# Static expert capacity of 608 rows in place of 640 in a fused attention, feed-forward and mixture-of-experts kernel

## The chip, the cores and the metric

The kernel runs on one core of one Trainium2 chip. The metric is the device time of one execution in microseconds, as the median of several runs. The profile is of one further execution on the same kind of core.

## The reference

Three stages follow on each other. First a landmark attention over 4 batches, 8 heads, 576 positions and head width 64 (32 landmarks, six steps of an iterative inverse). Its output, as 2304 tokens of width 512, goes through a feed-forward layer with an ELU (512 to 2048 to 512). The result `x` goes through eight experts, of which each token takes the two with the largest noisy logits:

```python
logits = x @ w_gate
noise_scale = np.log1p(np.exp(x @ w_noise))
noisy_logits = logits + noise_scale * noise
top2 = np.argpartition(-noisy_logits, 2, axis=1)[:, :2]
...
for e in range(E):
    for k in range(2):
        mask = top2[:, k] == e
        h = np.maximum(x[mask] @ w1[e], 0.0)
        out[mask] += top2_w[mask, k, None] * (h @ w2[e])
```

`w1[e]` is 512 x 1024 and `w2[e]` is 1024 x 512, with E = 8. 2304 tokens with two experts each make 4608 rows, 576 per expert on average; how many an expert gets depends on the inputs.

## The kernel before

All matrix products run in f16 with a split: a value is kept as a high half and a low half, and a product is three matmuls (high by high, high by low, low by high) summed in PSUM.

**Order of the work.** The Tile framework places the instructions, but from the attention to the end of expert 0 their order on every engine is written out by hand in the string ORDER, inside a manual schedule (line 1025). Experts 1 to 7 follow in a second manual schedule, the loop at line 1028. SP issues the plain DMAs and the transposing DMAs, POOL the indirect ones (gather and scatter by a list of row numbers).

**Routing.** As the tokens of a chunk come out of the feed-forward layer, the two experts of each token and its position in each expert's list are computed, and `RS` (line 837) scatters the token's row (512 values as two f16 halves, then token number, first expert and the two weights) into the DRAM table `xs`. Each expert has a section of STRIDE rows there. `fill_xs` (line 715) has earlier written zero rows with dummy token numbers over the first CAP = 640 rows of each section, so an expert always handles 640 rows, real ones and dummies. `count` holds the real row counts, `blocks` the number of blocks of 128 rows that lie past CAP.

**One expert.** `fetch_x` (line 869) brings its rows in transposed, as `XT[e]` (two halves, each 128 partitions by 4 by 640 columns), and their weights and token numbers as `WS[e]`. `weigh_x` (line 881) makes integer token numbers `TK[e]` and the right weight of each row. `ew_load` (line 853) loads expert weights two experts ahead in eight pieces of 512 KB; `ew_split` (line 858) splits each piece on ACT (high) and DVE (low).

The first layer is `e1` (line 913). For each of eight blocks `f` of 128 hidden columns it does two parts of the rows, 320 each: `e1_mm` (line 895) runs 12 matmuls (3 passes by 4 slices of the width) whose stationary operand is a 128 x 128 block of `w1` and whose moving operand is the part's columns of `XT`. Then `e1_hi` (line 903) applies ReLU on ACT and writes the high half of the hidden tile `EH[e, f]`, and `e1_lo` (line 908) makes the low half on DVE. Expert 0 is cut otherwise: its rows 0 to 383 (EARLY) are certain to be filled before the last chunk is routed, so its parts are 384 and 256 rows (`XP`, `EPART`, lines 1001 and 1002), and the second part is done after the last rows have been scattered.

The second layer is `e2` (line 939), over five blocks `j` of 128 rows. `e2_mm` (line 922) runs 24 matmuls (8 blocks f by 3 passes), in which the stationary operand is the 128 rows of the hidden tile and the moving operand is 512 columns of `w2`:

```python
for f in range(8):
    for i, (x, y) in enumerate(((0, 0), (0, 1), (1, 0))):
        T.matmul(p, EH[e, f][:, x, 128 * j:128 * j + 128], W2T[e][y][:, f, :],
```

`e2_out` (line 929) scales the 128 x 512 result by the row weights on ACT, and `e2_add` (line 933) adds it to the DRAM table `acc` with an indirect DMA that accumulates. The last expert is different: `last_base` (line 954) copies `acc` to the output and gathers the sums of its own rows, and each block is then weighted and added to those on DVE (line 946) and scattered straight into the output (line 948).

**The end.** From `peak` (line 1046) on, a branch handles experts with more than CAP real rows, 128 rows at a time, weights loaded and split anew. With no such expert the branch is skipped.

Of the kernel before, what the change touches and what calls it, by code (L numbers as in the profile page):

```python
# [8 lines left out]
F32 = mybir.dt.float32  # L9
F16 = mybir.dt.float16  # L10
I32 = mybir.dt.int32
U32 = mybir.dt.uint32
AF = mybir.ActivationFunctionType
ALU = mybir.AluOpType
# [6 lines left out]
DM, DFF = 512, 2048  # L21
NE, FE = 8, 1024
NT = B * S
CAP = 640
EARLY = 384
PITCH = 520
STRIDE = NT + 128
NT5 = 6
# [153 lines left out]
def attn_ffn_moe_kernel(ctx: ExitStack, tc: tile.TileContext, q: bass.AP, k: bass.AP, v: bass.AP,  # L182
                        w_in: bass.AP, w_out: bass.AP, w_gate: bass.AP, w_noise: bass.AP,
                        noise: bass.AP, w1: bass.AP, w2: bass.AP, out: bass.AP):
    nc = tc.nc
# [5 lines left out]
    cst = ctx.enter_context(tc.tile_pool(name="cst", bufs=1))  # L191
    sb = ctx.enter_context(tc.tile_pool(name="sb", bufs=1))
    ps = ctx.enter_context(tc.tile_pool(name="ps", bufs=1, space=bass.MemoryType.PSUM))
# [6 lines left out]
    V, A, G, T = nc.vector, nc.scalar, nc.gpsimd, nc.tensor  # L200
    PASSES = ((0, 0), (0, 1), (1, 0))

    def half(name):
        return sb.tile([128, 4096], F16, tag="half", bufs=12, name=name)
# [10 lines left out]
    def act(o, i, f=AF.Copy, **kw):  # L215
        return A.activation(o, i, f, **kw)  # L216
# [468 lines left out]
    blocks = cst.tile([128, NE], I32, name="blocks")  # L685
    counti = cst.tile([128, NE + 1], I32, name="counti")
    spacer = cst.tile([1, 1], F32, name="spacer")
    xs = dr.tile([NE * STRIDE, PITCH], F32, name="xs")
    acc = dr.tile([NT + 128, DM], F32, name="acc")

    wgf = {}
    zrow = cst.tile([128, PITCH], F32, name="zrow")
# [20 lines left out]
        V.tensor_scalar(zrow[:, DM:DM + 1], tokid[:, 0:1], float(NT), None, op0=ALU.add)  # L713

    def fill_xs(e):
        nc.sync.dma_start(xs[e * STRIDE:e * STRIDE + CAP].rearrange("(j p) c -> p j c", p=128),
                          zrow[:, None, :].to_broadcast([128, CAP // 128, PITCH]))

    def fill_acc(i):
        a = acc.rearrange("(j p) c -> p j c", p=128)[:, 5 * i:min(5 * i + 5, 19)]  # L720
# [15 lines left out]
    def routing(c):  # L736
# [75 lines left out]
        def RF():  # L812
# [16 lines left out]
            if c == LAST:  # L829
# [3 lines left out]
                V.tensor_copy(counti, count)  # L833
                V.tensor_scalar(blocks, count[:, :NE], float(CAP), float(127 - CAP), op0=ALU.max, op1=ALU.add)
                V.tensor_scalar(blocks, blocks, 7, None, op0=ALU.logical_shift_right)
# [13 lines left out]
    W1T, W2T, XT, WS, TK = {}, {}, {}, {}, {}  # L849
# [18 lines left out]

    def fetch_x(e, s0, s1_):
        if e not in XT:  # L870
            XT[e] = [half(f"xT{e}{i}")[:, :4 * CAP].rearrange("p (d n) -> p d n", d=4) for i in range(2)]
            WS[e] = cst.tile([128, CAP // 128, 4], F32, tag="ws", bufs=2, name=f"ws{e}")
            TK[e] = cst.tile([128, CAP // 128], I32, tag="tk", bufs=2, name=f"tk{e}")
        j0, j1 = s0 // 128, s1_ // 128
        src = xs[e * STRIDE + s0:e * STRIDE + s1_]
        for i in range(2):
            nc.sync.dma_start_transpose(out=XT[e][i][:, :, s0:s1_],
                                        in_=src[:, DM // 2 * i:DM // 2 * (i + 1)].bitcast(F16))
        nc.sync.dma_start(WS[e][:, j0:j1], src[:, DM:DM + 4].rearrange("(j p) c -> p j c", p=128))

    def weigh_x(e, s0, s1_):
        j0, j1 = s0 // 128, s1_ // 128
        w = WS[e][:, j0:j1]
        V.tensor_copy(TK[e][:, j0:j1, None], w[:, :, 0:1])
        V.scalar_tensor_tensor(w[:, :, 2:3], w[:, :, 1:2], float(e), w[:, :, 2:3], op0=ALU.is_equal,
                               op1=ALU.mult)
        V.scalar_tensor_tensor(w[:, :, 3:4], w[:, :, 1:2], float(e), w[:, :, 3:4], op0=ALU.not_equal,
                               op1=ALU.mult)
        V.tensor_tensor(out=w[:, :, 2:3], in0=w[:, :, 2:3], in1=w[:, :, 3:4], op=ALU.add)

    EH = {}
# [3 lines left out]
    def e1_mm(e, f, s0, n):  # L895
        tag = ("l1", "a")[f % 2 if e == 0 else s0 > 0]
        p = EP[e, f, s0] = ps.tile([128, 512], F32, tag=tag, bufs=2, name=f"eh{e}_{f}_{s0}")[:, :n]
        for i, (x, y) in enumerate(((0, 0), (0, 1), (1, 0))):
            for d in range(4):
                T.matmul(p, W1T[e][x][:, d, 128 * f:128 * f + 128], XT[e][y][:, d, s0:s0 + n],  # L900
                         start=(i == 0 and d == 0), stop=(i == 2 and d == 3))

    def e1_hi(e, f, s0, n):
        if (e, f) not in EH:
            EH[e, f] = sbe.tile([128, 2, CAP], F16, tag="hT", bufs=8, name=f"eh{e}_{f}")
        act(EH[e, f][:, 0, s0:s0 + n], EP[e, f, s0], AF.Relu)
# [6 lines left out]
    def e1(e, f, parts):  # L913
        for s0, n in parts:
            for g in (e1_mm, e1_hi, e1_lo):
                g(e, f, s0, n)

    outs, BASE = [], {}

    EY = {}  # L920

    def e2_mm(e, j):
        p = EY[e, j] = ps.tile([128, 512], F32, tag="y", bufs=3, name=f"ey{e}_{j}")
        for f in range(8):
            for i, (x, y) in enumerate(((0, 0), (0, 1), (1, 0))):
                T.matmul(p, EH[e, f][:, x, 128 * j:128 * j + 128], W2T[e][y][:, f, :],  # L926
                         start=(f == 0 and i == 0), stop=(f == 7 and i == 2))

    def e2_out(e, j):
        o = EO[e, j] = sb.tile([128, DM], F32, tag="t5", bufs=NT5, name=f"eo{e}_{j}")  # L930
        act(o, EY[e, j], scale=WS[e][:, j, 2:3])

    def e2_add(e, j):
        nc.gpsimd.indirect_dma_start(out=acc[:, :], out_offset=bass.IndirectOffsetOnAxis(ap=TK[e][:, j:j + 1], axis=0),  # L934
                                     in_=EO[e, j], in_offset=None, compute_op=ALU.add)

    EO = {}

    def e2(e, j):
        e2_mm(e, j)  # L940
        if e < NE - 1:
            e2_out(e, j)
            e2_add(e, j)
            return
        o = sb.tile([128, DM], F32, tag="t5", bufs=NT5, name=f"eo{e}_{j}")
        V.scalar_tensor_tensor(o, EY[e, j], WS[e][:, j, 2:3], BASE[j], op0=ALU.mult, op1=ALU.add)
        G.memset(spacer, 0.0)
        n = nc.gpsimd.indirect_dma_start(out=out[:, :], out_offset=bass.IndirectOffsetOnAxis(ap=TK[e][:, j:j + 1], axis=0),  # L948
                                         in_=o, in_offset=None, bounds_check=NT - 1, oob_is_err=False)
        for x in outs:  # L950
            tc.declare_no_dep(n.ins, x.ins, reason="a row of its own")
        outs.append(n)

    def last_base(e):
        nc.sync.dma_start(out, acc[:NT])
        for j in range(CAP // 128):
            BASE[j] = sb.tile([128, DM], F32, tag="t5", bufs=NT5, name=f"base{j}")
            nc.gpsimd.indirect_dma_start(out=BASE[j], out_offset=None, in_=acc[:, :],
                                         in_offset=bass.IndirectOffsetOnAxis(ap=TK[e][:, j:j + 1], axis=0))


    def step(g, n=1):
# [26 lines left out]
    def pool():  # L989
# [6 lines left out]
           "consts": route_consts, "cl": route_loads, "PD": ew_load, "P": ew_split,  # L996
           "LX": lambda e, p: fetch_x(e, *XP[e][p]), "LW": lambda e, p: weigh_x(e, *XP[e][p]),
           "E1": lambda f, p: e1_mm(0, f, *EPART[p]), "EA": lambda f, p: e1_hi(0, f, *EPART[p]),
           "EV": lambda f, p: e1_lo(0, f, *EPART[p]), "E2": lambda j: e2_mm(0, j), "EO": lambda j: e2_out(0, j),
           "ES": lambda j: e2_add(0, j), "pool": pool, "F": warm}  # L1000
    XP = {0: ((0, EARLY), (EARLY, CAP)), 1: ((0, CAP),)}
    EPART = ((0, EARLY), (EARLY, CAP - EARLY))
    for n in "XTSHO":
        CMD[n] = lambda c, f, *e, n=n: elu(c, f, n, *e)
# [22 lines left out]
    manual.enter_context(tc.manual_schedule(engines={ET.PE, ET.DVE, ET.Activation, ET.Pool, ET.SP}))  # L1027
    for e in range(1, NE):
        if e + 1 < NE:
            fetch_x(e + 1, 0, CAP)  # L1030
        if e == NE - 1:
            last_base(e)
        for f in range(8):
            e1(e, f, [(0, CAP // 2), (CAP // 2, CAP // 2)])
            if e + 1 < NE:
                for part in range(2):
                    ew_split(e + 1, f, part)
            if e + 2 < NE:
                ew_load(e + 2, f)
        for j in range(5):  # L1040
            e2(e, j)
            if j == 1 and e + 1 < NE:
                weigh_x(e + 1, 0, CAP)
    manual.close()

    peak = nc.values_load(counti[0:1, NE:NE + 1], min_val=0, max_val=NT)  # L1046
    with tc.If(peak > CAP):
        ef = cst.tile([128, 1], F32, name="ef")
        V.memset(ef, -1.0)
        with tc.For_i(0, NE, 1) as e:  # L1050
            V.tensor_scalar(ef, ef, 1.0, None, op0=ALU.add)
            nb = nc.values_load(blocks[0:1, bass.ds(e, 1)], min_val=0, max_val=(NT - CAP) // 128)
            with tc.If(nb > 0):
                ce = nc.values_load(counti[0:1, bass.ds(e, 1)], min_val=0, max_val=NT)
                nc.sync.dma_start(xs[bass.ds(e * STRIDE + ce, 128)], zrow)
# [2 lines left out]
                for src, dst, kn, nm, scale in ((w1, w1x, 1, "a", S_W1), (w2, w2x, 2, "b", S_W2)):  # L1058
                    for j in range(4):
# [6 lines left out]
                                               op1=ALU.subtract)  # L1066
                with tc.For_i(0, nb, 1) as i:
# [5 lines left out]
                    tk = cst.tile([128, 1], I32, name="tkx")  # L1073
# [3 lines left out]
                                           op1=ALU.mult)  # L1077
                    V.tensor_tensor(out=wt[:, 2:3], in0=wt[:, 2:3], in1=wt[:, 3:4], op=ALU.add)
                    base = sb.tile([128, DM], F32, tag="t5", bufs=NT5, name="basex")
# [5 lines left out]
                    for f in range(8):  # L1085
                        p = ps.tile([128, 512], F32, tag="l1", bufs=2, name=f"hx{f}")[:, :128]
# [6 lines left out]
                    p = ps.tile([128, 512], F32, tag="y", bufs=3, name="yx")  # L1093
# [36 lines left out]
```

## Time and profile before

| | |
|---|---|
| median of 3 runs | 853.97 us (853.81 to 853.98) |
| profiled execution, its own time | 854.51 us |
| its span, first to last instruction | 852.8 us |
| mean granted TensorE clock over the span | 0.977 |
| instructions in the span | 15270 |

The time of an execution and the span of its profile differ by what lies around the first and last instruction, here 1.7 us. PE is TensorE's matmuls and PEld its weight loads, which overlap them; DVE, ACT and POOL are the vector, scalar and GpSimd engines, and SPq is the queue that issues DMAs. In a group of the profile "busy" is the union of its instructions' times, the mean is that of one instruction, and the idle time is that of the engine just before them, with what ended it. A matmul's mean is longer than the distance from one to the next, because matmuls are pipelined. "128*128 128x320" is a stationary operand of 128 x 128 and a moving one of 320 columns. The timeline merges neighbours of the same kind: start, length from the first start to the last end, and count.

### The profile page before, as it was taken

The numbers are of one execution on the slowest core, as the hardware profiler recorded it, in microseconds if no ns is written. First come the engines' busy times: TensorE is split into PE (matmuls) and PEld (weight loads), VectorE is DVE, ScalarE is ACT, GpSimd is POOL, SyncE is SP. The second block draws the span as 40 slices with busy tenths as digits, with TensorE's granted clock in tenths as the row PEclk, the third lists the DMA queues.
The fourth block names the chain that finished last, engine by engine and source line by source line (L and its number), as shares of the span: only waits on it lengthen the run. The fifth ranks groups of instructions, "written<-read, shape, count | busy, mean of one in ns | idle before, by whom it ended". The sixth has DMA issues, their size and how long they took to land. (4 is left out here: it accounts for less than half of the span.)

```text
span 852.8 us, 15270 instructions
## 1 busy us (share of the span) xinstructions
PE 807.9 (95%) x6113; PEld 470.0 (55%) x6114; DVE 449.1 (53%) x984; ACT 409.2 (48%) x749; POOL 294.5 (35%) x313
## 2 busy tenths in 40 slices
PE   7768989999999999999999999999999999999994
PEld 6653345555654556654456664746557465564752
DVE  7989999876684974636461340613416043160210
ACT  5677668776757576565532341514325143241200
POOL 4556755665552454354430212021020210202311
PEclk9769999999999999999999999999999999999997
DMA  9868699597486513341659876565646747403730
GB/s 341 300 155 192 181 324 343 138 222 222 90 208 122 193 46 110 107 109 49 181 151 171 142 189 84 148 149 111 171 67 163 144 113 185 51 2 40 221 110 35
DMA packets 137227, 129.64 MB, mean 152 GB/s; under 512 B 100597, under 2 KB 103669, under 8 KB 137056
## 3 DMA queue, kind: packets, MB, share of 16 engines
q1 hardware_dynamic: 128432, 107.32, 47.5%
q0 software_dynamic: 8720, 21.30, 11.8%
q8 instruction: 49, 0.80, 0.4%
q14 instruction: 26, 0.21, 0.1%
HBM read 70.71 MB, written 40.42 MB: 130 GB/s over the span
## 5 line engine op out<-in xcount | busy, mean ns | idle before, releaser
L900 PE MATMUL eh<-xT,w 128*128 128x320 f16 (+2 forms) x1536 | 210.6, 299 | 0.0
L926 PE MATMUL ey<-w,eh 128*128 128x512 f16 x960 | 208.8, 379 | 0.0
L671 PE MATMUL y<-wout,g 128*128 128x512 f16 x864 | 207.0, 379 | 0.7 <-POOL g L664 0.7
L910 DVE SCALAR_TENSOR_TENSOR eh<-eh,eh 128x320 f16<-128x320 f32 (+2 forms) x128 | 62.0, 489 | 236.8 <-ACT eh L216 236.8
L900 PEld LDWEIGHTS <-w 128*128 128x128 f16 x1536 | 150.1, 98 | 59.7
L926 PEld LDWEIGHTS <-eh 128*128 128x128 f16 x960 | 93.9, 98 | 111.7
L934 POOL DMA_INDIRECT acc<-eo,tk x35 | 54.6, 1561 | 290.6 <-ACT eo L216 157.0
L664 POOL TENSOR_TENSOR g<-e,g 128x384 f16<-128x384 f32 (+2 forms) x96 | 100.6, 1051 | 129.1 <-ACT g L216 114.0
L671 PEld LDWEIGHTS <-g 128*128 128x128 f16 x864 | 81.3, 99 | 93.5 <-issue 8.3
L633 PE MATMUL h<-AT,G 128*128 128x192 f16 (+3 forms) x768 | 110.1, 289 | 8.1 <-DVE e L659 5.0
L216 ACT ACTIVATE eh<-eh 128x320 f16<-128x320 f32 (+2 forms) x128 | 55.5, 437 | 126.6 <-PE eh L900 117.1
L633 PEld LDWEIGHTS <-G 128*128 128x128 f16 x768 | 64.2, 99 | 49.6 <-issue 11.2
L867 DVE SCALAR_TENSOR_TENSOR w<-ew,w 128x1024 f16<-128x1024 f32 x64 | 78.2, 1224 | 22.0 <-ACT w L216 22.0
L216 ACT ACTIVATE eo<-ey,ws 128x512 f32<-128x512 f32 x35 | 23.8, 688 | 135.0 <-PE ey L926 135.0
L659 DVE SCALAR_TENSOR_TENSOR e<-e,h 128x384 f32<-128x384 f32 (+2 forms) x96 | 52.7, 550 | 32.1 <-ACT e L216 21.4
L216 ACT ACTIVATE e<-h 128x384 f32<-128x384 f32 (+2 forms) x96 | 47.2, 493 | 46.3 <-PE h L633 22.4
L216 ACT ACTIVATE w<-ew 128x1024 f16<-128x1024 f32 x64 | 67.0, 1048 | 0.0
L216 ACT ACTIVATE g<-e 128x384 f16<-128x384 f32 (+2 forms) x96 | 49.7, 519 | 32.6 <-DVE e L659 18.0
L839 POOL DMA_INDIRECT xs<-rows,pos x36 | 36.5, 1014 | 31.5 <-DVE count L831 20.5
L216 ACT ACTIVATE e<-e 128x384 f32<-128x384 f32 (+2 forms) x57 | 29.9, 524 | 0.9
L655 DVE TENSOR_SCALAR e<-e 128x384 f32<-128x384 f32 (+2 forms) x39 | 19.2, 492 | 16.8 <-ACT e L216 16.7
L608 DVE SCALAR_TENSOR_TENSOR G<-pg,G 128x512 f16<-128x512 f32 x32 | 21.6, 690 | 7.8 <-ACT G L216 7.8
(199 smaller groups left out, 753.8 us busy)
## 6 DMA issues: line engine op xcount, KB each, us to landing
ew<-in_moe_w_dram SPq DMA_DIRECT2D x64, 512.0 KB, 3.7
xs<-zrow SPq DMA_DIRECT2D x8, 1300.0 KB, 19.2
wo<-in_moe_w_out_dram SPq DMA_DIRECT2D x16, 512.0 KB, 4.5
wi<-in_moe_w_in_dram SPq DMA_DIRECT2D x16, 512.0 KB, 8.3
q<-in_q_dram SPq DMA_DIRECT2D x8, 576.0 KB, 7.1
k<-in_k_dram SPq DMA_DIRECT2D x8, 576.0 KB, 6.3
v<-in_v_dram SPq DMA_DIRECT2D x4, 1152.0 KB, 13.0
out_dram<-acc SPq DMA_DIRECT2D x1, 4608.0 KB
```

The source lines that it names most:

```text
L216: return A.activation(o, i, f, **kw)
L608: V.scalar_tensor_tensor(gt[:, g, 1, fs], X["pg"][g], S_G, gt[:, g, 0, fs], op0=ALU.mult, op1=ALU.subtract)
L633: T.matmul(p[:, c0:c0 + n], GT[b, f // 8][:, g, x, fs], AT[b][:, g, y, o:o + n], start=(i == 0), stop=(i == 5))
L659: V.scalar_tensor_tensor(x[1], x[1], x[2], x[0], op0=ALU.mult, op1=ALU.max)
L664: G.tensor_tensor(out=HT[c, f][:, 1], in0=x[1], in1=HT[c, f][:, 0], op=ALU.subtract)
L671: T.matmul(YP[c, t], h[:, x, 128 * t:128 * t + 128], WOUT[f][:, y], start=(f == 0 and i == 0), stop=(f == 15 and i == 2))
L839: n = nc.gpsimd.indirect_dma_start(out=xs[:, :], out_offset=bass.IndirectOffsetOnAxis(ap=R["pos"][:, i // 2, i % 2:i % 2 + 1], axis=0), in ...
L867: V.scalar_tensor_tensor(dst[1][:, ks, :], t, scale, dst[0][:, ks, :], op0=ALU.mult, op1=ALU.subtract)
L900: T.matmul(p, W1T[e][x][:, d, 128 * f:128 * f + 128], XT[e][y][:, d, s0:s0 + n], start=(i == 0 and d == 0), stop=(i == 2 and d == 3))
L910: V.scalar_tensor_tensor(h[:, 1, s0:s0 + n], EP[e, f, s0], 0.0, h[:, 0, s0:s0 + n], op0=ALU.max, op1=ALU.subtract)
L926: T.matmul(p, EH[e, f][:, x, 128 * j:128 * j + 128], W2T[e][y][:, f, :], start=(f == 0 and i == 0), stop=(f == 7 and i == 2))
L934: nc.gpsimd.indirect_dma_start(out=acc[:, :], out_offset=bass.IndirectOffsetOnAxis(ap=TK[e][:, j:j + 1], axis=0), in_=EO[e, j], in_offset= ...
```

## The change

The capacity CAP becomes 608. A new constant PAD = 640 takes its place where rows are filled, fetched, weighed and transposed, so that these handle as many rows as before. The two parts of a first layer are 304 columns each for experts 1 to 7 and 384 and 224 for expert 0. The five blocks of a second layer stay; a new function `live(j)` gives the rows of block j, which are 128 for the first four and 96 for the last. The last block's matmuls take 96 columns of the hidden tile as stationary operand, and its eviction, its scatter and, for the last expert, its gather handle 96 rows. The hidden tile has 608 columns. The branch at the end is taken if an expert has more than 608 rows, and its bound on blocks is rounded up.

```diff
--- before.py
+++ after.py
@@ -21,7 +21,8 @@
 DM, DFF = 512, 2048
 NE, FE = 8, 1024
 NT = B * S
-CAP = 640
+CAP = 608
+PAD = 640
 EARLY = 384
 PITCH = 520
 STRIDE = NT + 128
@@ -713,8 +714,8 @@
         V.tensor_scalar(zrow[:, DM:DM + 1], tokid[:, 0:1], float(NT), None, op0=ALU.add)
 
     def fill_xs(e):
-        nc.sync.dma_start(xs[e * STRIDE:e * STRIDE + CAP].rearrange("(j p) c -> p j c", p=128),
-                          zrow[:, None, :].to_broadcast([128, CAP // 128, PITCH]))
+        nc.sync.dma_start(xs[e * STRIDE:e * STRIDE + PAD].rearrange("(j p) c -> p j c", p=128),
+                          zrow[:, None, :].to_broadcast([128, PAD // 128, PITCH]))
 
     def fill_acc(i):
         a = acc.rearrange("(j p) c -> p j c", p=128)[:, 5 * i:min(5 * i + 5, 19)]
@@ -868,9 +869,9 @@
 
     def fetch_x(e, s0, s1_):
         if e not in XT:
-            XT[e] = [half(f"xT{e}{i}")[:, :4 * CAP].rearrange("p (d n) -> p d n", d=4) for i in range(2)]
-            WS[e] = cst.tile([128, CAP // 128, 4], F32, tag="ws", bufs=2, name=f"ws{e}")
-            TK[e] = cst.tile([128, CAP // 128], I32, tag="tk", bufs=2, name=f"tk{e}")
+            XT[e] = [half(f"xT{e}{i}")[:, :4 * PAD].rearrange("p (d n) -> p d n", d=4) for i in range(2)]
+            WS[e] = cst.tile([128, PAD // 128, 4], F32, tag="ws", bufs=2, name=f"ws{e}")
+            TK[e] = cst.tile([128, PAD // 128], I32, tag="tk", bufs=2, name=f"tk{e}")
         j0, j1 = s0 // 128, s1_ // 128
         src = xs[e * STRIDE + s0:e * STRIDE + s1_]
         for i in range(2):
@@ -919,19 +920,23 @@
 
     EY = {}
 
+    def live(j):
+
+        return min(128, CAP - 128 * j)
+
     def e2_mm(e, j):
-        p = EY[e, j] = ps.tile([128, 512], F32, tag="y", bufs=3, name=f"ey{e}_{j}")
+        p = EY[e, j] = ps.tile([128, 512], F32, tag="y", bufs=3, name=f"ey{e}_{j}")[:live(j)]
         for f in range(8):
             for i, (x, y) in enumerate(((0, 0), (0, 1), (1, 0))):
-                T.matmul(p, EH[e, f][:, x, 128 * j:128 * j + 128], W2T[e][y][:, f, :],
+                T.matmul(p, EH[e, f][:, x, 128 * j:128 * j + live(j)], W2T[e][y][:, f, :],
                          start=(f == 0 and i == 0), stop=(f == 7 and i == 2))
 
     def e2_out(e, j):
-        o = EO[e, j] = sb.tile([128, DM], F32, tag="t5", bufs=NT5, name=f"eo{e}_{j}")
-        act(o, EY[e, j], scale=WS[e][:, j, 2:3])
+        o = EO[e, j] = sb.tile([128, DM], F32, tag="t5", bufs=NT5, name=f"eo{e}_{j}")[:live(j)]
+        act(o, EY[e, j], scale=WS[e][:live(j), j, 2:3])
 
     def e2_add(e, j):
-        nc.gpsimd.indirect_dma_start(out=acc[:, :], out_offset=bass.IndirectOffsetOnAxis(ap=TK[e][:, j:j + 1], axis=0),
+        nc.gpsimd.indirect_dma_start(out=acc[:, :], out_offset=bass.IndirectOffsetOnAxis(ap=TK[e][:live(j), j:j + 1], axis=0),
                                      in_=EO[e, j], in_offset=None, compute_op=ALU.add)
 
     EO = {}
@@ -942,10 +947,10 @@
             e2_out(e, j)
             e2_add(e, j)
             return
-        o = sb.tile([128, DM], F32, tag="t5", bufs=NT5, name=f"eo{e}_{j}")
-        V.scalar_tensor_tensor(o, EY[e, j], WS[e][:, j, 2:3], BASE[j], op0=ALU.mult, op1=ALU.add)
+        o = sb.tile([128, DM], F32, tag="t5", bufs=NT5, name=f"eo{e}_{j}")[:live(j)]
+        V.scalar_tensor_tensor(o, EY[e, j], WS[e][:live(j), j, 2:3], BASE[j], op0=ALU.mult, op1=ALU.add)
         G.memset(spacer, 0.0)
-        n = nc.gpsimd.indirect_dma_start(out=out[:, :], out_offset=bass.IndirectOffsetOnAxis(ap=TK[e][:, j:j + 1], axis=0),
+        n = nc.gpsimd.indirect_dma_start(out=out[:, :], out_offset=bass.IndirectOffsetOnAxis(ap=TK[e][:live(j), j:j + 1], axis=0),
                                          in_=o, in_offset=None, bounds_check=NT - 1, oob_is_err=False)
         for x in outs:
             tc.declare_no_dep(n.ins, x.ins, reason="a row of its own")
@@ -953,10 +958,10 @@
 
     def last_base(e):
         nc.sync.dma_start(out, acc[:NT])
-        for j in range(CAP // 128):
-            BASE[j] = sb.tile([128, DM], F32, tag="t5", bufs=NT5, name=f"base{j}")
+        for j in range(PAD // 128):
+            BASE[j] = sb.tile([128, DM], F32, tag="t5", bufs=NT5, name=f"base{j}")[:live(j)]
             nc.gpsimd.indirect_dma_start(out=BASE[j], out_offset=None, in_=acc[:, :],
-                                         in_offset=bass.IndirectOffsetOnAxis(ap=TK[e][:, j:j + 1], axis=0))
+                                         in_offset=bass.IndirectOffsetOnAxis(ap=TK[e][:live(j), j:j + 1], axis=0))
 
 
     def step(g, n=1):
@@ -998,7 +1003,7 @@
            "E1": lambda f, p: e1_mm(0, f, *EPART[p]), "EA": lambda f, p: e1_hi(0, f, *EPART[p]),
            "EV": lambda f, p: e1_lo(0, f, *EPART[p]), "E2": lambda j: e2_mm(0, j), "EO": lambda j: e2_out(0, j),
            "ES": lambda j: e2_add(0, j), "pool": pool, "F": warm}
-    XP = {0: ((0, EARLY), (EARLY, CAP)), 1: ((0, CAP),)}
+    XP = {0: ((0, EARLY), (EARLY, PAD)), 1: ((0, PAD),)}
     EPART = ((0, EARLY), (EARLY, CAP - EARLY))
     for n in "XTSHO":
         CMD[n] = lambda c, f, *e, n=n: elu(c, f, n, *e)
@@ -1027,7 +1032,7 @@
     manual.enter_context(tc.manual_schedule(engines={ET.PE, ET.DVE, ET.Activation, ET.Pool, ET.SP}))
     for e in range(1, NE):
         if e + 1 < NE:
-            fetch_x(e + 1, 0, CAP)
+            fetch_x(e + 1, 0, PAD)
         if e == NE - 1:
             last_base(e)
         for f in range(8):
@@ -1040,7 +1045,7 @@
         for j in range(5):
             e2(e, j)
             if j == 1 and e + 1 < NE:
-                weigh_x(e + 1, 0, CAP)
+                weigh_x(e + 1, 0, PAD)
     manual.close()
 
     peak = nc.values_load(counti[0:1, NE:NE + 1], min_val=0, max_val=NT)
@@ -1049,7 +1054,7 @@
         V.memset(ef, -1.0)
         with tc.For_i(0, NE, 1) as e:
             V.tensor_scalar(ef, ef, 1.0, None, op0=ALU.add)
-            nb = nc.values_load(blocks[0:1, bass.ds(e, 1)], min_val=0, max_val=(NT - CAP) // 128)
+            nb = nc.values_load(blocks[0:1, bass.ds(e, 1)], min_val=0, max_val=(NT - CAP + 127) // 128)
             with tc.If(nb > 0):
                 ce = nc.values_load(counti[0:1, bass.ds(e, 1)], min_val=0, max_val=NT)
                 nc.sync.dma_start(xs[bass.ds(e * STRIDE + ce, 128)], zrow)
```

## Rows read from the trace of the kernel before

**Rows 1.** The page: span, engines' busy time, slices of PE and its clock
```profile
span 852.8 us, 15270 instructions
...
PE 807.9 (95%) x6113; PEld 470.0 (55%) x6114; DVE 449.1 (53%) x984; ACT 409.2 (48%) x749; POOL 294.5 (35%) x313
...
PE   7768989999999999999999999999999999999994
...
PEclk9769999999999999999999999999999999999997
```

**Rows 2.** Windows: busy us of PE, PEld, DVE, ACT, POOL, then clock, DMA, GB/s
```profile
437.00:842.00 405.00, 404.43 (x2435) 237.23 (x2432) 128.25 (x235) 122.25 (x206) 70.81 (x60) 1.00 0.57 125
...
529.40:555.40 26.00, 26.00 (x193) 18.75 (x192) 15.27 (x22) 13.85 (x23) 1.56 (x1) 1.00 0.57 143
```

**Rows 3.** Groups from 437 to 842 us: busy us, mean ns, idle us before, releasers
```profile
L926 PE MATMUL ey<-w,eh 128*128 128x512 f16 x960 | 208.8, 379 | 0.0
L900 PE MATMUL eh<-xT,w 128*128 128x320 f16 x1344 | 183.9, 299 | 0.0
...
L926 PEld LDWEIGHTS <-eh 128*128 128x128 f16 x960 | 93.9, 98 | 111.7
...
L216 ACT ACTIVATE w<-ew 128x1024 f16<-128x1024 f32 x49 | 51.4, 1048 | 0.0
...
L900 PE MATMUL eh<-xT,w 128*128 128x256 f16 x96 | 10.6, 273 | 0.0
...
L900 PE MATMUL eh<-xT,w 128*128 128x384 f16 x24 | 4.1, 326 | 0.0
```

**Rows 4.** Timeline of PE, the expert stage: start us, length us, what, count
```profile
423.50 7.96 PE L900 MATMUL eh<-xT,w 128*128 128x384 f16 x48
...
456.57 10.64 PE L900 MATMUL eh<-xT,w 128*128 128x256 f16 x96
467.05 2.11 PE L926 MATMUL ey<-w,eh 128*128 128x512 f16 x9
468.99 1.79 PE L900 MATMUL eh<-xT,w 128*128 128x320 f16 x12
...
503.49 26.06 PE L926 MATMUL ey<-w,eh 128*128 128x512 f16 x120
529.39 26.24 PE L900 MATMUL eh<-xT,w 128*128 128x320 f16 x192
```

**Rows 5.** Groups of the whole span, line 633, the form with 192 columns
```profile
L633 PE MATMUL h<-AT,G 128*128 128x192 f16 x288 | 28.8, 246 | 0.0
```

**Rows 6.** Timeline of PE near 330 us
```profile
329.63 1.15 PE L633 MATMUL h<-AT,G 128*128 128x192 f16 x12
```

**Rows 7.** Timeline near 116 us: loads and matmuls of line 488
```profile
116.40 0.46 PEld L488 LDWEIGHTS pe<-ident,E 128*96 128x96 f32 x4
116.51 0.60 PE L488 MATMUL pe<-ident,E 128*96 128x128 f32 x4
```

**Rows 8.** Line 488 by itself: duration ns least/median/most, first and last start, form
```profile
L488 PEld LDWEIGHTS pe<-ident,E x48: 124/126/210, 41.5 to 271.0; 128*96 128x96 f32 x48
```

**Rows 9.** Timeline of POOL: two scatter-adds that follow each other
```profile
626.35 1.56 POOL L934 DMA_INDIRECT acc<-eo,tk  x1 [3.94 <-DMA acc<-eo,tk]
631.72 1.56 POOL L934 DMA_INDIRECT acc<-eo,tk  x1 [3.81 <-DMA acc<-eo,tk]
```

**Rows 10.** Timeline of the last expert: copy, first scatter, last DVE operation
```profile
796.61 0.61 SPq L955 DMA_DIRECT2D out_dram<-acc  x1
...
821.78 1.02 POOL L948 DMA_INDIRECT out_dram<-eo,tk  x1 [18.17 <-DVE eo L946]
...
841.47 0.75 DVE L946 SCALAR_TENSOR_TENSOR eo<-ey,ws,base 128x512 f32<-128x512 f32 x1 [4.43 <-PE ey L926]
```

**Rows 11.** Timeline of SP near 454 us
```profile
453.60 8.59 SPq L877 DMA_TRANSPOSE xT<-xs  x2
```

**Rows 12.** Line 877 by itself, 437 to 842 us: time from issue to landing
```profile
DMA to landing us min/median/max: 4.0/6.7/9.2
```

## The prediction

> **What bounds the kernel now.** I read the page first. TensorE (PE) is busy 95% of the span and no other engine over 55%; the slices show PE at 9 from the seventh on and its clock at 9 from the fourth on, both but for the last slice [rows 1]. That is an average, so I asked by stage next. [...] Within one first layer (529.4 to 555.4) DVE has 15.3 and ACT 13.9 of 26.0 us [rows 2]. In the groups of that stage the idle time ahead of every PE matmul group is 0.0 [rows 3]: no transfer, eviction or weight load is waited for. So in this stage the time is the number of matmuls times the spacing of their starts, and the change is in this stage alone. (Most first-layer matmuls of expert 0 on its columns 0 to 383 lie just ahead; they are untouched.)
>
> **The spacing of a matmul.** The mean duration in a group is no price, since matmuls overlap. The spacing comes from the timeline, as the length of a stretch less one duration, over its count less one.
> - 384 columns: (7.96 - 0.326)/47 = 162.4 ns; 320: (26.24 - 0.299)/191 = 135.8 ns; 256: (10.64 - 0.273)/95 = 109.1 ns [rows 3, 4].
> - 192 columns, in another stage: (1.15 - 0.246)/11 = 82.2 ns [rows 5, 6].
>
> From 192 to 384 each column costs 0.42 ns, and no floor shows down to 192. A weight load takes 98 ns [rows 3] beside each matmul, which even at the 82.2 costs nothing that can be seen.
>
> **The change, part by part.**
> 1. *First layer of experts 1 to 7, 304 for 320 columns.* 7 experts x 8 column blocks x 2 halves x 12 = 1344 matmuls, the count of the group [rows 3]. One column is (162.4 - 109.1)/128 = 0.416 ns, so each loses 16 x 0.416 = 6.66 ns: 1344 x 6.66 = 8.95 us, all on PE's unbroken path.
> 2. *Second part of expert 0, 224 for 256 columns.* 96 matmuls [rows 4], 32 x 0.416 = 13.3 ns each (224 lies between the measured 192 and 256): 1.28 us.
> 3. *Last block of every second layer, 96 for 128 rows.* The rows are columns of the stationary operand; the moving operand is still 512 wide. These are 24 matmuls x 8 experts = 192, now (26.06 - 0.379)/119 = 215.8 ns apart, with a 98 ns load beneath [rows 3, 4]. No f16 matmul with 96 stationary columns runs before. The nearest is the f32 transpose at line 488: four loads of 96 columns start (0.46 - 0.126)/3 = 111 ns apart and four matmuls fit in 0.60 us with them [rows 7, 8]. So a 96-column load keeps pace with matmuls half as far apart as the 215.8. A gain is excluded, because the 512 columns that stream are unchanged. I take 0, by that nearest row; the upper end is a load not hidden at all, 192 x 98 ns = 18.8 us (first rival).
> 4. *Evictions, splits and other work on ACT and DVE.* 304 columns make the evictions a little shorter. PE's time covers them already [rows 2]: 0. A first layer then has 24.97 us for DVE's 15.3, so the cover holds.
> 5. *Scatter-adds.* Five per expert on POOL; each waits until the one before it has landed, 5.4 us apart [rows 9], some 27 us in an expert of 52 us (twice the 25.9 us from 503.49 to 529.39) [rows 4]: 0, and still 0 at 50.7 us. The last of the five moves 96 rows.
> 6. *Fills, fetches of rows, their transposes, and weights* keep 640 rows under the name PAD, so SP issues the same list: 0. For the last expert the copy of the sums to the output is issued at 796.61 and the first scatter into the output leaves 25.2 us later, after an idle time that is put down to DVE and not to the copy [rows 10]. The scatter comes 1.3 us sooner relative to the copy. If the copy were then late, its remainder would show at most that 1.3 us on POOL, beside PE's four more blocks: 0.
> 7. *The tail.* PE's last result is taken by DVE at 841.47 (0.75 us), then come a scatter of about 1.0 us like the first and the closing steps, to 852.8 [rows 1, 10]. The last scatter has 96 rows for 128: at best a quarter of 1.0, 0.25 us; at worst nothing. I take 0, since the closing steps are longer than the scatter and do not hang on its rows.
>
> **Sum:** 8.95 + 1.28 = 10.23 us. The profiled execution took 854.51 us, 1.7 over its span; it becomes 844.28. The median of the three runs is 853.97, 0.54 lower; with the same difference the forecast is **843.7 us**, 1.2% less.
>
> **Rivals.**
> *The narrow load is not hidden (slower).* Place: the 192 matmuls of part 3. If a 96-column load cannot run beneath the matmul ahead of it, each adds up to 98 ns, 18.8 us in all: 853.97 - 10.23 + 18.8 = 862.5. It turns the sign from 10.23/192 = 53 ns of exposure, which a hidden load reaches if it grows from 98 to 269 ns. For it: the form is new here. Against it: the 96-column f32 loads, which take about 126 ns and keep pace at 111 [rows 7, 8]. Chance 0.04.
> [...] No row here shows an f16 load of 96 columns.
>
> *The seam between experts 0 and 1 gives part back.* SP issues the two transposes of expert 1's rows from 453.60 on, in 8.59 us [rows 11]. If the second goes out halfway, at 457.9, then with 4.0, 6.7 or 9.2 us to landing (least, median, most) [rows 12] it lands at 461.9, 464.6 or 467.1. The first matmuls that read them start at 468.99 [rows 4]; 1.28 us sooner that is 467.7, so most of the reserve against the worst landing is gone. They stand behind nine matmuls of expert 0's second layer [rows 4], a place that the scheduler chose where two hand-written stretches meet. If they move ahead of those nine, they ask at 467.05 - 1.28 = 465.8 and wait up to 1.3 us, with all later work of PE behind them; 843.7 to 845.0, or some 846 if a later landing adds to it. For it: the small reserve. Against: there is no wait there now, and at the median landing none would arise. Chance 0.10.
>
> *The spacing does not follow the columns,* so that the change fails to shorten PE's work: at most the 1.28 us of part 2 is left, 852.7, no change by measure. The four spacings speak against it. Chance 0.01.
>
> *An expert has more than 608 rows.* Then the overflow loop, skipped now, runs at the end. Eight weight splits of 1.05 us on ACT [rows 3], 96 matmuls of 128 columns at about 82.2 - 64 x 0.42 = 55 ns and 24 of 215.8 ns follow on each other: 8.4 + 5.3 + 5.2 = 18.9 us at least, so 862.6 or more. But the two largest noisy logits of every token, counted from the inputs by the reference's formula, give 583, 594, 559, 539, 580, 583, 573 and 597 rows; the largest is 11 below 608. Chance 0.01.
>
> **How the numbers follow.** The sum has 0.84, the seam 0.10, the load 0.04, the other two 0.01 each. The range starts 0.9 below the sum: 0.25 for the tail, 0.2 between runs, the rest for a small shift of the stages ahead, where the clock still changes [rows 1]. It ends at the seam's worst, 846.0. What is left out is the load, the spacing and the overflow, 0.06, and some spread. A measurement of this kernel can tell 0.2% (1.7 us) from no change. Faster by more than that holds for sum and seam, 0.94; within it the spacing, 0.01; slower the load and the overflow, 0.05.
>
> **What would show it.** Right: first layers of 192 matmuls in 24.97 us (26.24 - 1.28), expert 0's 96 matmuls in some 9.36, second layers still 26.06, no idle time ahead of any matmul group of the stage, loads of 96 columns under 216 ns, and still 11.4 us from DVE's last operation to the end of the span. Wrong: second layers over 26.1 us (the load); a wait for a transpose at line 900 near 467 us (the seam); a spacing at 304 columns other than 135.8 - 6.7 = 129.1 ns; matmuls after line 1046 (overflow).

## The result and the profile after

| | before | after |
|---|---|---|
| median | 853.98 us (853.81 to 856.03, 4 runs) | 844.09 us (843.73 to 844.50, 4 runs) |
| ratio, 95% interval | | 0.9871 (0.9858 to 0.9884) |
| profiled execution, and its span | 854.51 us, 852.8 us | 843.73 us, 842.1 us |

The kernel is 9.9 us faster; the forecast was 843.7 us, 10.2 us less. The page of the changed kernel, as [rows 1]:

```profile
span 842.1 us, 15270 instructions
...
PE 796.1 (95%) x6113; PEld 473.4 (56%) x6114; DVE 446.9 (53%) x984; ACT 407.6 (48%) x749; POOL 295.3 (35%) x313
...
PE   7768989999999999999999999999999999999994
...
PEclk9869999999999999999999999999999999999998
```

The slices look alike and PE keeps its 95%: a shorter stage of the same kind. PE's busy time fell by 11.8 us, about 1 us more than the span; that rest lies ahead of the experts (from 38 to 100 us PE was busy 50.5 us at a mean granted clock of 0.83 before, and 49.5 at 0.86 after). The windows of the changed kernel, as [rows 2] (busy time of PE, PEld, DVE, ACT and POOL, clock, share of the DMA engines, GB/s), over the expert stage and over one first layer:

```profile
437.00:831.40 394.40, 393.64 (x2423) 241.39 (x2421) 125.74 (x231) 119.96 (x206) 72.11 (x60) 1.00 0.58 127
526.30:551.10 24.80, 24.80 (x194) 18.79 (x193) 14.97 (x22) 13.65 (x23) 1.44 (x1) 1.00 0.61 147
```

PE is still without a gap in a first layer, at a granted clock of 1.00, with DVE at 15.0 us of 24.8. The groups of the changed kernel in the expert stage, as [rows 3] (busy us, mean ns, idle us before):

```profile
L901 PE MATMUL eh<-xT,w 128*128 128x304 f16 x1344 | 174.9, 293 | 0.0
L931 PE MATMUL ey<-w,eh 128*128 128x512 f16 x768 | 167.4, 379 | 0.0
...
L931 PEld LDWEIGHTS <-eh 128*128 128x128 f16 x768 | 75.1, 98 | 88.9
...
L931 PE MATMUL ey<-w,eh 128*96 128x512 f16 x192 | 42.7, 379 | 0.0
L931 PEld LDWEIGHTS <-eh 128*96 128x96 f16 x192 | 23.6, 123 | 18.0
```

The 1344 matmuls of the first layers fell from 183.9 to 174.9 us of busy time, 9.0 us. The second layers' groups are 167.4 and 42.7 for 208.8 before; the two figures overlap where one kind follows on the other. One row is new: a load of 96 columns lasts 123 ns, longer than the 98 of a load of 128. The timeline of PE in the changed kernel, as [rows 4], shows whether that is paid for:

```profile
422.96 7.96 PE L901 MATMUL eh<-xT,w 128*128 128x384 f16 x48
...
456.02 9.36 PE L901 MATMUL eh<-xT,w 128*128 128x224 f16 x96
465.22 2.11 PE L931 MATMUL ey<-w,eh 128*128 128x512 f16 x9
467.16 1.71 PE L901 MATMUL eh<-xT,w 128*128 128x304 f16 x12
...
551.08 26.06 PE L931 MATMUL ey<-w,eh 128*128 128x512 f16 x120
576.98 24.96 PE L901 MATMUL eh<-xT,w 128*128 128x304 f16 x192
```

A first layer takes 24.96 us for 26.24, expert 0's second part 9.36 for 10.64, and a second layer with its narrow block the same 26.06 (the row merges both kinds). It is not paid for. The two transposes of expert 1's rows, line 878 from 453 to 462 us (count, duration in ns, first and last start; least, median and most from issue to landing, of which 8.1 us is the first's and 5.6 the second's):

```profile
L878 SPq DMA_TRANSPOSE xT<-xs x2: 3599/4092/4585, 453.0 to 457.7; - x2
DMA to landing us min/median/max: 5.6/6.8/8.1
```

And at the end of the changed kernel, as [rows 10] (timeline: copy to the output, first scatter, last DVE operation, last scatter):

```profile
786.14 0.62 SPq L960 DMA_DIRECT2D out_dram<-acc  x1
...
810.99 1.03 POOL L953 DMA_INDIRECT out_dram<-eo,tk  x1 [17.84 <-DVE eo L951]
...
830.68 0.75 DVE L951 SCALAR_TENSOR_TENSOR eo<-ey,ws,base 96x512 f32<-96x512 f32 x1 [4.43 <-PE ey L931]
831.71 0.93 POOL L953 DMA_INDIRECT out_dram<-eo,tk  x1 [4.13 <-DVE eo L951]
```

The last scatter of the kernel before, in the same view:

```profile
842.50 0.98 POOL L948 DMA_INDIRECT out_dram<-eo,tk  x1 [4.13 <-DVE eo L946]
```

From the first expert matmul to DVE's last operation it was 841.47 - 423.50 = 417.97 us [rows 4, 10] and is 830.68 - 422.96 = 407.72: 10.25 us less. What is left after it is 11.4 us in both. The other 0.54 us by which the profiled executions differ arose ahead of the first expert matmul, where the order of the work is the same.

That stretch is the measure of the experiments, since what lies ahead of it differs between the profiled executions by some 2.5 us. From the timelines (us; the stretch and the rest are worked out to 0.01 from unrounded starts):

| kernel | first expert matmul | last DVE operation on an expert's rows | stretch | from there to the end |
|---|---|---|---|---|
| before | 423.50 | 841.47 | 417.96 | 11.36 |
| after | 422.96 | 830.68 | 407.72 | 11.37 |
| first layers alone | 425.12 | 832.83 | 407.72 | 11.37 |
| last block alone | 423.55 | 841.51 | 417.96 | 11.37 |
| quarters, 96 columns | 425.51 | 834.67 | 409.16 | 11.37 |
| quarters, 128 columns | 424.03 | 833.19 | 409.16 | 11.37 |
| capacity 600 | 423.30 | 828.46 | 405.16 | 11.37 |
| capacity 592 | 423.35 | 825.94 | 402.60 | 105.15 |
| eighths, 96 columns | 425.49 | 860.76 | 435.27 | 11.37 |
| eighths, 128 columns | 425.51 | 837.93 | 412.42 | 11.37 |
| sixteenths, 96 columns | 424.52 | 1022.29 | 597.77 | 11.37 |
| sixteenths, 128 columns | 425.18 | 876.48 | 451.30 | 11.37 |
| sixteenths, 64 columns | 424.14 | 889.34 | 465.20 | 11.35 |

### The profile page after: what moved, and what is told of

It reads as the page before. It is cut to its first block, busy times and chain, and to the rows that moved or that the text cites. A ratio compares the mean times of both kernels' runs of the same rounds, so it can differ in the third digit from the quotient of the medians.

```text
span 842.1 us, 15270 instructions
## 1 busy us (share of the span) xinstructions
PE 796.1 (95%) x6113; PEld 473.4 (56%) x6114; DVE 446.9 (53%) x984; ACT 407.6 (48%) x749; POOL 295.3 (35%) x313
## 5 line engine op out<-in xcount | busy, mean ns | idle before, releaser
L931 PE MATMUL ey<-w,eh 128*128 128x512 f16 (+1 forms) x960 | 208.8, 379 | 0.0
L901 PE MATMUL eh<-xT,w 128*128 128x304 f16 (+2 forms) x1536 | 200.4, 293 | 0.0
L911 DVE SCALAR_TENSOR_TENSOR eh<-eh,eh 128x304 f16<-128x304 f32 (+2 forms) x128 | 59.8, 471 | 228.0 <-ACT eh L217 228.0
L931 PEld LDWEIGHTS <-eh 128*128 128x128 f16 (+1 forms) x960 | 98.7, 103 | 106.9
L939 POOL DMA_INDIRECT acc<-eo,tk x35 | 55.9, 1597 | 280.2 <-ACT eo L217 144.1
L217 ACT ACTIVATE eh<-eh 128x304 f16<-128x304 f32 (+2 forms) x128 | 53.8, 424 | 118.0 <-PE eh L901 111.3
L217 ACT ACTIVATE eo<-ey,ws 128x512 f32<-128x512 f32 (+1 forms) x35 | 23.8, 687 | 135.1 <-PE ey L931 135.1
L217 ACT ACTIVATE e<-h 128x384 f32<-128x384 f32 (+2 forms) x96 | 47.4, 495 | 47.3 <-PE h L634 22.0
L217 ACT ACTIVATE g<-e 128x384 f16<-128x384 f32 (+2 forms) x96 | 49.8, 520 | 31.7 <-DVE e L660 18.6
```

What stands on the lines that cost most here:

```text
L911: V.scalar_tensor_tensor(h[:, 1, s0:s0 + n], EP[e, f, s0], 0.0, h[:, 0, s0:s0 + n], op0=ALU.max, op1=ALU.subtract)
L931: T.matmul(p, EH[e, f][:, x, 128 * j:128 * j + live(j)], W2T[e][y][:, f, :], start=(f == 0 and i == 0), stop=(f == 7 and i == 2))
```

## The experiments

The theory: the expert stage lasts as long as its matmuls are spaced, the spacing follows the streamed columns alone, and a stationary block narrower by 32 columns neither gives nor costs. The main rival: the narrow load takes time from PE. Spacings below are (busy - 8 x mean)/(count - 8), since each of the eight experts' blocks ends with one whole duration.

**First layers alone.** All matmuls of the second layer load 128 columns again.

```diff
-T.matmul(p, EH[e, f][:, x, 128 * j:128 * j + live(j)], W2T[e][y][:, f, :],
+T.matmul(p, EH[e, f][:, x, min(128 * j, CAP - 128):min(128 * j + 128, CAP)], W2T[e][y][:, f, :],
```

> Only the first layers keep their 304 and 224 columns; the last block of a second layer again loads 128 columns as stationary operand (rows 480 to 607 of the hidden tile), and its first 96 result rows are stored as rows 512 to 607, so the rows of that block are wrong. My theory (the whole gain is the streamed columns, the 96-column block costs and gives nothing): 844.1 us, within 0.5 of the changed kernel, first layers of experts 1 to 7 in 24.96 us, second layers 26.06. Rival (the narrow load, 123 ns in the changed kernel against 98, is partly paid for): up to 192 x 25 ns = 4.8 us faster than the changed kernel, 839.3. Second rival (the narrow block itself gives something): slower than the changed kernel by what it gave.

Measured: 846.14 us, 2.0 us over the 844.1 expected. The kernel before had 855.69 on that chip, a ratio of 0.9889 (0.9872 to 0.9906); the 0.9871 of the whole change lies just outside this interval, and the two intervals overlap. The stretch tells the two apart better: it is 407.72 us, that of the changed kernel to 0.01, and what is longer here lies ahead of the first expert matmul, at 425.12 us for 422.96. The group of this kernel, all 960 matmuls again of one kind:

```profile
L931 PE MATMUL ey<-w,eh 128*128 128x512 f16 x960 | 208.8, 379 | 0.0
```

So the whole gain is there without the narrow block, and the narrow block costs nothing.

**Last block alone.** The first layers go back to 320 and 256 columns, the last block keeps 96 rows.

```diff
-EPART = ((0, EARLY), (EARLY, CAP - EARLY))
+EPART = ((0, EARLY), (EARLY, PAD - EARLY))
-EH[e, f] = sbe.tile([128, 2, CAP], F16, tag="hT", bufs=8, name=f"eh{e}_{f}")
+EH[e, f] = sbe.tile([128, 2, PAD], F16, tag="hT", bufs=8, name=f"eh{e}_{f}")
-e1(e, f, [(0, CAP // 2), (CAP // 2, CAP // 2)])
+e1(e, f, [(0, PAD // 2), (PAD // 2, PAD // 2)])
```

> Only the last block of the second layers keeps its 96 rows (matmuls, evictions, scatters); the first layers again run 320 and 320 columns, and 384 and 256 for expert 0. My theory: as the kernel before, 854.0 us, at best 0.3 less by the shorter last scatter; first layers 26.24 us, second layers 26.06. Rival (the narrow load is partly paid for): up to 4.8 us slower, 858.8. Second rival (the narrow block gives something): faster than 853.5.

Measured: 854.77 us where the kernel before had 855.69 on that chip, ratio 0.9995 (0.9985 to 1.0005), no difference. The stretch is 417.96 us, as before to 0.01. Its groups have both the old first layer and the new block:

```profile
L901 PE MATMUL eh<-xT,w 128*128 128x320 f16 x1344 | 183.9, 299 | 0.0
...
L931 PE MATMUL ey<-w,eh 128*96 128x512 f16 x192 | 42.7, 379 | 0.0
```

**How much of a narrow load does a matmul hide?** The 123 ns of the new row asked for it. The last block's 512 moving columns were cut into passes of w = 128, 64 and 32, each with its own loads, so that less and less streams over a load:

```diff
+for c in range(0, 512, w if j == 4 else 512):
+    cs = slice(c, c + (w if j == 4 else 512))
...
-T.matmul(p, EH[e, f][:, x, 128 * j:128 * j + live(j)], W2T[e][y][:, f, :],
+T.matmul(p[:, cs], EH[e, f][:, x, 128 * j:128 * j + live(j)], W2T[e][y][:, f, cs],
```

The base line of each width loads 128 columns, by the edit of the first experiment. Quarters (w = 128):

> The changed kernel, but the last block of every second layer runs its 512 moving columns as four passes of 128, each with its own loads of 96 stationary columns, so 768 matmuls in place of 192. It asks how much of a 96-column load a short matmul still hides. If a narrow load takes no more of PE than a load of 128 columns, 128 moving columns are spaced at some 56 ns (135.8 less 192 x 0.416), 768 x 56 = 43.0 us, 1.6 us over the 41.4 of the changed kernel: 845.7. If the 25 ns by which its duration is longer are PE's own time, the spacing is up to 81 ns, 62.2 us: some 865. If a 96-column load does not overlap a matmul at all (123 + 56 ns): 137 us, some 940, but then the changed kernel could not have kept its 216 ns.

> The same four passes of 128 moving columns, but with loads of 128 stationary columns (rows 480 to 607; the rows of that block are wrong, as in the run that keeps the first layers alone). All theories: spacing 56 ns, 768 x 56 = 43.0 us, 845.7. It is the base line for the narrow load: the difference between the two runs, over 768, is what a 96-column load costs beyond one of 128 when only 128 columns stream over it.

Measured: 847.72 and 846.24 us in one run each, the difference ahead of the experts (425.51 and 424.03); the stretch is 409.16 us in both. The block in the first of the two:

```profile
L933 PE MATMUL ey<-w,eh 128*96 128x128 f16 x768 | 44.2, 219 | 0.0
...
L933 PEld LDWEIGHTS <-eh 128*96 128x96 f16 x768 | 44.0, 123 | 1.7
```

and in the second:

```profile
L933 PE MATMUL ey<-w,eh 128*128 128x128 f16 x768 | 44.2, 219 | 0.0
```

Both spacings are (44.2 - 1.75)/760 = 55.9 ns, so 128 streamed columns hide the narrow load in full, a quarter of what the change has. Eighths (w = 64), to see what a load of 96 columns takes of PE beneath so short a matmul:

> The last block's 512 moving columns in eight passes of 64, each with loads of 96 stationary columns: 1536 matmuls. The quarters showed 55.8 ns for 128 moving columns with either load. Here 64 columns stream in 29 ns. [...] If it takes no more than the load of 128 columns: 29.3 ns, 45.0 us, and the expert stage is 407.68 + 3.6 = 411.3 us, 847.7 in all. If the 25 ns of longer duration are paid: 54 ns, 83 us, some 886.

> The base line of the eighths: the same passes of 64 moving columns with loads of 128 stationary columns (rows 480 to 607; the rows of the last block are wrong). Both theories: 29.3 ns, as line 633 has with 64 columns, 1536 x 29.3 = 45.0 us, the stage at 411.3 us.

Measured: 873.81 and 850.98 us, in one run each. The block's matmuls with 96 stationary columns:

```profile
L933 PE MATMUL ey<-w,eh 128*96 128x64 f16 x1536 | 70.3, 209 | 0.0
```

and with 128:

```profile
L933 PE MATMUL ey<-w,eh 128*128 128x64 f16 x1536 | 47.4, 193 | 0.1
```

The spacings are (70.3 - 1.67)/1528 = 44.9 and (47.4 - 1.54)/1528 = 30.0 ns. Here the narrow load shows, with 14.9 ns; its spacing is neither the 29.3 ns nor the 54 of the expectation. The stage of the base line is 1.1 us longer than expected, most of it in the spacing, 30.0 ns for 29.3; the cause of that is open. Sixteenths (w = 32), and a load of 64 columns, were to tell a floor that goes with the load's columns from a fixed addition:

> The last block in sixteen passes of 32 moving columns with loads of 96 stationary columns: 3072 matmuls. With 64 moving columns a 96-column load made the spacing 44.9 ns against 30.0 with 128 stationary columns. Theory A (the load occupies PE for some 45 ns, and a matmul hides it only if it streams for longer): 44.9 ns again, 3072 x 44.9 = 137.9 us, the expert stage at 407.7 - 41.4 + 137.9 = 504.2 us. Theory B (a fixed 15 ns are added to each short matmul): less, some 25 + 15 = 40 ns, 489 us.

> The base line: 32 moving columns with loads of 128 stationary columns (rows 480 to 607; the last block's rows are wrong). Both theories: about 25 ns, as line 751 of the kernel before has with 32 columns; 76.8 us, the stage at 443 us.

> The same sixteen passes of 32 moving columns, with loads of 64 stationary columns (rows 512 to 575; rows 576 to 607 of every expert are left out). Loads lasted 117, 120 and 123 ns for 80, 88 and 96 columns, 0.38 ns a column. Theory A (the load occupies PE in proportion to its columns): 44.9 - 32 x 0.4 = 32 ns, 98 us, the stage at 464.5 us. Theory B (a fixed addition for any load of fewer than 128 columns): the spacing of the 96-column run.

For the last, the rows of the block were cut as well:

```diff
-return min(128, CAP - 128 * j)
+return min(128, CAP - 32 - 128 * j)
```

Measured: 1035.35, 889.53 and 902.46 us, in one run each. The load of 64 columns came as theory A had it:

```profile
L933 PE MATMUL ey<-w,eh 128*64 128x32 f16 x3072 | 98.7, 183 | 0.0
```

(98.7 - 1.46)/3064 = 31.7 ns (32 expected), the stretch 465.20 (464.5). With 128 stationary columns the group is

```profile
L933 PE MATMUL ey<-w,eh 128*128 128x32 f16 x3072 | 80.5, 176 | 3.8 <-issue 3.6
```

which is a spacing of 25.8 ns with 3.8 us of gaps on top, put down to issue. The stretch, 451.3 us, is some 8 us over what was expected: 2.5 for a spacing of 25.8 in place of 25 ns, 3.8 for the gaps, and 2.0 in the first layers (176.6 us of busy time and 0.3 of idle time for 174.9). One of these took 26.45 us for 24.96; gaps of 0.5 and 0.9 us lie in the narrow passes just ahead of it, and from 652 to 656 us, at its start, the mean granted clock was 0.64. With 96 columns the stretch was 597.8 us, 94 over theory A, and the windows of that kernel show why (three stretches: the first within the narrow passes of one expert, the second, but for its last 1.2 us, in the first four blocks of the next, the third at the start of that expert's narrow passes; columns as in [rows 2]):

```profile
478.00:502.00 24.00, 24.00 (x302) 23.90 (x301) 0.47 (x1) 0.46 (x2) 1.56 (x1) 0.50 0.09 13
526.50:548.00 21.50, 21.50 (x123) 10.43 (x121) 2.09 (x6) 3.89 (x6) 4.68 (x3) 1.00 0.70 141
546.90:551.50 4.60, 4.60 (x107) 4.60 (x105) 0.00 (x0) 0.69 (x1) 1.22 (x1) 1.00 0.43 56
```

In the first window the granted clock was 0.50, though PE counts as busy all the time; in the next blocks it was back at 1.00, and it was still 1.00 as the next narrow passes began. The groups of the first window:

```profile
L933 PE MATMUL ey<-w,eh 128*96 128x32 f16 x300 | 24.2, 241 | 0.0
L933 PEld LDWEIGHTS <-eh 128*96 128x96 f16 x298 | 24.0, 195 | 0.0
```

(24.2 - 0.24)/299 = 80 ns. And of the third window, at a granted clock of 1.00:

```profile
L933 PE MATMUL ey<-w,eh 128*96 128x32 f16 x106 | 4.9, 196 | 0.0
```

(4.9 - 0.20)/105 = 44.8 ns, the 44.9 of theory A. So theory A holds at a clock of 1.00, at 0.50 the spacing is 1.8 times as long, and what was missed is that the clock itself fell. Of the 94 us, 84 lie in the narrow passes (221.8 us of busy time for the 137.9 of theory A) and some 11 in the first layers that follow them (185.9 us for 174.9), at the start of which the clock is still low: in the one that begins at 573.63 it is 0.50 from 574 to 578 us and 0.87 from 578 to 582.

**Capacity 600.** One number, CAP = 600, against the kernel before.

> Capacity 600 in place of 608: halves of 300 columns, 216 in expert 0's second part, a last block of 88 rows; the largest count is 597, so the overflow loop stays skipped. My theory (the time of the expert stage is the streamed columns alone): 1344 x 4 x 0.416 = 2.24 us and 96 x 8 x 0.416 = 0.32 us less than the changed kernel, 2.56 in all; from the first matmul of expert 0 to the last of expert 7 405.12 us (407.68 in the changed kernel), and 841.5 us for the whole where the changed kernel has 844.1. Rival (a spacing goes by steps or alignment, and 300 columns cost as much as 304): 407.4 to 407.7 for the stage.

Measured: 842.17 us (841.50 to 843.40) for 854.56 of the kernel before on that chip, ratio 0.9859 (0.9838 to 0.9880). The stretch by the expectation's measure, first to last matmul, is the 405.16 of the table less 0.04 between last matmul and DVE, 405.12 us, as forecast. Its groups:

```profile
L901 PE MATMUL eh<-xT,w 128*128 128x300 f16 x1344 | 172.7, 291 | 0.0
L931 PE MATMUL ey<-w,eh 128*128 128x512 f16 x768 | 167.4, 379 | 0.0
L931 PE MATMUL ey<-w,eh 128*88 128x512 f16 x192 | 42.7, 379 | 0.0
...
L931 PEld LDWEIGHTS <-eh 128*88 128x88 f16 x192 | 23.0, 120 | 18.6
```

There is no step and no effect of alignment at 300 and 216 columns. Against the changed kernel the gain is 2.56 us in the stage; the two ratios to the kernel before have overlapping intervals, so the whole time does not tell them apart. By its stretch it is the fastest version here whose overflow loop stays skipped, with 3 rows left above the largest count.

**Capacity 592.** The other side: two experts now have more rows than the capacity.

> Capacity 592: experts 1 and 7 have 594 and 597 rows, so the loop at the end runs for two experts, one block each. It prices the other side of the capacity. The expert stage by my theory: 407.68 - 2 x 2.56 = 402.56 us. Then the loop: at least 18.9 us for each of the two (eight splits of 1.05 us, 96 and 24 matmuls), and before that the loading of 4 MB of weights, at the 341 GB/s of the best slice some 12 us, plus eight steps of reading a count: 62 us and more in all, so some 905, and in any case slower than both kernels. If the loads, splits and matmuls ran beside each other: two times 12 us, some 865.

Measured: 932.84 us in one run. The stretch is 402.60 us (402.56 from first to last matmul, as forecast), and the part after it grew from 11.4 to 105.2. Its narrow loads, of 80 columns:

```profile
L931 PEld LDWEIGHTS <-eh 128*80 128x80 f16 x192 | 22.5, 117 | 19.1
```

In the timeline of that kernel, the step that opens each turn of the overflow loop on DVE, and the first matmuls of a turn:

```profile
827.11 0.15 DVE L1056 TENSOR_SCALAR ef<-ef 128x1 f32<-128x1 f32 x1 [0.33 <-DVE ef L1054]
839.24 0.15 DVE L1056 TENSOR_SCALAR ef<-ef 128x1 f32<-128x1 f32 x1 [11.97 <-PEq L1055]
...
855.72 2.72 PE L1094 MATMUL hx<-xtx,w1x 128*128 128x128 f16 x24 [29.82 <-DMA xtx<-xs]
...
875.47 0.15 DVE L1056 TENSOR_SCALAR ef<-ef 128x1 f32<-128x1 f32 x1 [6.18 <-PEq L1055]
879.54 0.15 DVE L1056 TENSOR_SCALAR ef<-ef 128x1 f32<-128x1 f32 x1 [3.92 <-PEq L1055]
```

Expert 1, with its one block of two rows, takes 875.47 - 839.24 = 36.2 us, 16.5 of them before the first matmul; the next turn, of an expert that is skipped, still takes 4.1 us, and the first turn 12.1. The expectation of 62 us and more was a lower bound; the loop cost 93.8 us, half as much again.

## Why the prediction was right

1. *The bound.* Read rightly. With PE's idle time at 0.0 in every matmul group of the first and second layers, the whole of the saved spacing came through: the stretch fell by 10.25 us for 10.23 forecast. The stretch holds one wait of PE, for DVE's routing work, just ahead of the stage that the prediction read, from 437 us on [rows 2, 3]: 0.86 us until 436.83 before and 0.85 us until 436.28 after. It lies ahead of every changed matmul and cancels.
2. *First layer, 8.95 us, and expert 0, 1.28 us.* The price of a column, from the spacings at 384 and 256 columns, held at 304, 300 and 224: a first layer of 24.96 us (24.97 forecast), expert 0's part of 9.36 (9.36). The first layers alone give the whole gain.
3. *Last block, 0.* Right in the sum: with the block alone the stretch is that of before to 0.01 us. In the working, the f32 row of 126 ns was the right neighbour for the duration (123) and the f16 row of 98 was not. The first rival's condition, a load not hidden, fails: to turn the sign the load would have to keep PE for 269 ns, and the eighths show that it keeps PE for 45.
   The narrow loads do last longer: those of 80, 88 and 96 columns last 117, 120 and 123 ns, some 0.4 ns a column, and a line through them would put 128 columns at some 135, where 98 is measured. None of it was paid for: with 512 streamed columns over them the stretches are 402.60, 405.16 and 407.72 us, as the streamed columns alone give.
4. *The seam.* It gave nothing back. The twelve matmuls stand behind the same nine and start 467.16 - 456.02 = 11.14 us after expert 0's second part, for 12.42 before [rows 4]: the 1.28 came through with no wait. The second transpose of expert 1's rows was issued at 457.7 and landed after 5.6 us, at 463.3, almost 4 us before those matmuls; the prediction had put the median landing at 464.6. The longest landing of these transposes in the stage, 8.8 us, would have left some 0.6 us. The kernels with capacities of 600 and 592 ask sooner still after expert 0's second part, and their stretches are as forecast to 0.01 us. So the reserve was there, but part of it was a short landing.
5. *Tail, 0.* The last scatter took 0.93 us for 0.98, less than a quarter of the 0.25 that 96 rows for 128 could have given, and the end came 11.4 us after DVE's last operation as before. In part 6 the scatter was to come 1.3 us sooner relative to the copy of the sums. It came 0.3 us sooner, 810.99 - 786.14 = 24.85 us for 25.17; why the copy moved along is open, and the term of 0 does not hang on it.
6. *Overflow.* Not taken at 608 and 600; taken at 592, as the counts said. The rival's floor of 18.9 us for an expert that overflows was about half of the 36.2 measured.

The median is 0.4 us over the forecast. In 13 profiles the first expert matmul starts between 422.96 and 425.51 us, although what lies ahead of it is the same work, while stretches that should be alike agree to 0.01 us. So the 0.4 us most likely lies ahead of the experts; that is not shown, since the profile is of one execution, which took 843.73 us. The clock still changes ahead of the experts (a mean of 0.86 from 38 to 100 us of the changed kernel, 1.00 from 100 to 150); which of its changes makes which difference was not tried.

## What to carry to other kernels

Where a stage's engine has no idle time ahead of any of its groups, a change in that stage can be priced from the spacing at two or three sizes: here 10.23 us for 10.25 measured. The spacing, and not the mean duration of an instruction, is the price (215.8 ns for a mean of 379 with 512 columns). Padding was paid for on the side that streams: 32 rows fewer gave 10.25 us where rows are the moving columns and nothing where they are the stationary ones (a stretch of 417.96 us as before). A static capacity gains 2.6 us for every 8 rows here and loses some 36 us for an expert that crosses it, and more for the loop itself (93.8 us in all with two such experts), so it goes down to the largest count that can occur and not below.

## What the runs showed of the hardware

Where the load showed in the spacing of the matmuls, 96 f16 columns took 44.8 ns and 64 took 31.7 at a granted clock of 1.00, and 96 took 80 ns at 0.50. From the first two an estimate is (44.8 - 31.7)/32 = 0.41 ns a column, about the 0.416 ns of a streamed column, and some 5 ns more. Matmuls that streamed 512 or 128 columns, 215.8 and 55.9 ns apart, hid the load of 96 wholly; those that streamed 64 were 44.9 ns apart over it for 30.0 over loads of 128, and those that streamed 32 were 44.8 for 25.8. Loads of 128 columns allowed a spacing of 25.8 ns in the sixteenths, so such a load kept PE for no more than that; whether the load or something else sets the 25.8 ns no run here separates.

And the granted clock fell to 0.50 in a stretch where PE was never idle by the profile (478 to 502 us of the sixteenths, 24.00 us busy of 24.00): passes of 32 moving columns over loads of 96. The same passes over loads of 64 ran at 1.00, with PE as busy (a stretch of 11 us in that kernel, columns as in [rows 2]):

```profile
530.00:541.00 11.00, 11.00 (x352) 11.00 (x350) 0.00 (x0) 0.40 (x1) 1.55 (x1) 1.00 0.33 48
```

Over loads of 128 the mean granted clock was 0.64 from 652 to 656 us, at the start of a first layer behind gaps of 0.5 and 0.9 us. So a PE that is busy by the profile was not enough to keep the clock up here; what it is about the passes over 96 columns that let it fall, no run separates.
